# Attention and a token and channel mixer: the last addition of each sum of exponentials by an accumulating DMA, the second channel weight rounded during attention, and the first token product by seven products

## The chip, the cores and the metric

The kernel runs on one core of a Trainium2 chip. The metric is the device time of one execution in microseconds, lower is better.

The profile tells the core's work by engine, here with the instructions of each in the kernel before: TensorE (PE, 3885; its weight loads PEld, 3885), VectorE (DVE, 881), ScalarE (ACT, 707), GpSimd (POOL, 77) and SyncE (SP), which here mostly issues transfers. What it calls the DMA share is the mean busy share of sixteen DMA engines.

## The reference

Hashed attention feeds a mixer of two stages:

```python
q, k, v: (4, 8, 768, 64)      # batch, heads, sequence, head dimension
mask   = bucket(q) == bucket(k)                  # six signs of a projection
scores = where(mask, q @ k.T / 8, -1e9)
attn   = exp(scores - max) / sum                 # (768 x 768 for each head)
x      = (attn @ v) as (4, 768, 512)

h = relu(x.T @ w_tok1) @ w_tok2                  # token mixing: 768 -> 256 -> 768
u = x + h.T
out = u + relu(u @ w_ch1) @ w_ch2                # channel mixing: 512 -> 1536 -> 512
```

The mixer's four weights arrive as 64-bit numbers and are rounded to 32 bits on the chip. This document calls that a conversion.

## The kernel before

Attention handles 16 pairs of heads, one after another. A pair has two halves of 384 queries, and a half has six blocks of keys. For each block TensorE makes scores in one of three buffers (`sc`), where a product with bit rows (`bits`) does the masking. ScalarE takes the exponential of the block, and VectorE adds the six blocks of a half to `esd`, whose column sums are the denominators. Between the two halves of one pair and the scores of the next, TensorE does the previous sums, the hash of the next pair, and the weighting of the values.

```python
class Half:
    ...
    def add(self):
        self.d = pool.tile([P, 2, HALF], F32, name="esd", tag="esd", bufs=4)
        nc.vector.scalar_tensor_tensor(self.d, es[0], NR * EPS, es[1], ...)
        for e in es[2:-1]:
            nc.vector.tensor_tensor(self.d, self.d, e, op=ALU.add)
    def add_last(self):
        nc.vector.tensor_tensor(self.d, self.d, self.es[-1], op=ALU.add)

def hashes(n):                    # makes the bit rows of pair n, during pair n - 1
    ...                           # four products into hp
    nc.vector.tensor_scalar(g, ps[:, :HALF], 0.0, 0.5, op0=ALU.is_gt, op1=ALU.subtract)
    nc.scalar.mul(g, g, bitscale)
    ...                           # then eight small transfers
        nc.sync.dma_start(out=bitrows[n % 2][...], in_=g[...])

for n in range(len(pairs)):
    ...
    for now in halves:
        now.scores(); now.add()
        if now.half == 0: now.add_last()
    before.sums()
    hashes(n + 1)
    halves[1].add_last()
    load_qk(n + 2)
    add_values(n)
    weights.begin()               # ScalarE step of one conversion
    before.newton()
    weights.join()                # four VectorE steps
    halves[0].weigh()
    before.divide()
    weights.turnover()            # last VectorE step, then the load of a further weight block
    halves[1].weigh()
    if n and n % 2 == 0: bounce(...)          # stores of x, transposed, for the token stage
    if n == 2 * NP: fetch(0, x0)  # 1.5 MB: batch 0 of x comes back, after pair 8
```

Pair n + 1 cannot mask its first score block until the eight transfers of `hashes` have landed. They are issued on SyncE.

In the token stage each batch had a first product of full size, a second product by seven products, and, between them, the conversions of `w_ch2`. (Seven products means the scheme in which a product of two 2 x 2 block matrices takes seven block products instead of eight, at the price of sums.)

Of the kernel before, what the change touches and what calls it, by code (L numbers as in the profile page):

```python
# [34 lines left out]
F32 = mybir.dt.float32  # L37
BF16 = mybir.dt.bfloat16
U32 = mybir.dt.uint32
I32 = mybir.dt.int32  # L40
I64 = mybir.dt.int64
ALU = mybir.AluOpType
ACT = mybir.ActivationFunctionType
# [5 lines left out]
def kernel(  # L49
# [91 lines left out]
    class Conversion:  # L141


        def __init__(self, pool, parts, bufs):
            self.pool, self.bufs = pool, bufs
            self.todo = [
                (w, dst, rows, j, n)
                for w, dst, rows, blocks in parts
                for j in range(*blocks, rows)
                for n in range(0, dst.shape[2], NW // rows)  # L150
            ]
            self.fetched, self.begun, self.ready = [], None, None
            for _ in range(bufs - 1):
                self.fetch()
# [25 lines left out]
        def join(self):  # L180
            if not self.begun:
                return
            raw, size, to, rows = self.begun
            self.begun = None
            unit = self.pool.tile([P, NW], F32, name="unit", tag="unit", bufs=1)

            nc.vector.tensor_scalar(
                unit.bitcast(U32), size.bitcast(U32), 3, 0x7F800000,
                op0=ALU.logical_shift_left, op1=ALU.bitwise_and,
            )  # L190
            nc.vector.tensor_scalar(
                size.bitcast(U32), size.bitcast(U32), 3, None, op0=ALU.logical_shift_left,
            )

            nc.vector.scalar_tensor_tensor(unit, raw[:, :, 0], 2.0**-52, unit, op0=ALU.mult, op1=ALU.mult)  # L195
            nc.vector.tensor_tensor(size, size, unit, op=ALU.add)  # L196
            self.ready = raw, size, to, rows

        def end(self):

            if not self.ready:
                return
            raw, size, to, rows = self.ready
            self.ready = None
            hi, size = (a.rearrange("p (t n) -> p t n", t=rows) for a in (raw[:, :, 1], size.bitcast(U32)))
            nc.vector.scalar_tensor_tensor(
                to.bitcast(U32), hi, 0x80000000, size, op0=ALU.bitwise_and, op1=ALU.bitwise_or,
            )

        def turnover(self):  # L210
# [13 lines left out]

    dram = ctx.enter_context(tc.tile_pool(name="dram", bufs=1, space=bass.MemoryType.DRAM))
    bounced = [dram.tile([S, DM], F32, name=f"bounced{b}") for b in range(B)]

# [30 lines left out]
    def attention(pool, psum, W1, W2, x0):  # L258
# [63 lines left out]
        class Half:  # L322
# [54 lines left out]
            def add_last(self):  # L377
                nc.vector.tensor_tensor(self.d, self.d, self.es[-1], op=ALU.add)  # L378

# [70 lines left out]
        for _ in range(12):  # L450
# [3 lines left out]
            pool,  # L454
            [(w_tok1, W1, 3, (0, NR)), (w_tok2, W2, 1, (0, NJ)), (w_ch1, WC1, 1, (0, NCB))],
            bufs=2,
# [4 lines left out]
        for n in range(len(pairs)):  # L461
# [3 lines left out]
            for now in halves:  # L465
# [4 lines left out]
                if now.half == 0:  # L470
                    now.add_last()
            if before:
                before.sums()
# [20 lines left out]
            if before:  # L494
                before.divide()
            weights.turnover()
            halves[1].weigh()
            if n and n % 2 == 0:
# [93 lines left out]

    def tokens(pool, psum, W1, W2, x0, weights, jobs, T, places):

# [5 lines left out]
        R1 = {}  # L600
        turned = not jobs
        if not turned:
            fetch(1, x1)
            jobs = jobs(weights(pool))
            bounce(places[2], len(pairs) - 2)
        NQ = DM // 2
        sums = pool.tile([P, 3, HALF], F32, name="W2sums", tag="W2sums", bufs=1)
        b00, b01, b10, b11 = (W2[:, k, HALF * n : HALF * n + HALF] for k in range(2) for n in range(2))

        def weight_sums():  # L610
            nc.vector.tensor_tensor(sums[:, 0], b01, b00, op=ALU.subtract)
            nc.vector.tensor_tensor(sums[:, 1], b11, sums[:, 0], op=ALU.subtract)
            nc.vector.tensor_tensor(b01, b11, b01, op=ALU.subtract)
            nc.vector.tensor_tensor(sums[:, 2], b10, sums[:, 1], op=ALU.subtract)

        def job():
            if not turned and jobs:
                jobs.pop(0)()

# [3 lines left out]
        def banks():  # L623
            return psum.tile([P, 2, 512], F32, name="trp", tag="tr", bufs=2)

        def mix1(b):
            x = (x0, x1)[b % 2]
            if b and turned:
                turn(b, x, banks)
            r1 = pool.tile([P, NJ, DM], F32, name="r1", tag="r1", bufs=2)  # L630
            for j in range(NJ):
                ps = bank("t1")
                for r in range(NR):
                    nc.tensor.matmul(  # L634
                        ps, W1[:, r, P * j : P * j + P], x[:, r], start=(r == 0), stop=(r == NR - 1),
                    )
                to = r1[:, j]
                if not turned:
                    to = to.rearrange("p (c g i) -> p g c i", c=NCB, i=32)
                    ps = ps.rearrange("p (g c i) -> p g c i", c=NCB, i=32)  # L640
                nc.scalar.activation(to, ps, ACT.Relu)
                job()
            if b % 2:
# [3 lines left out]
            R1[b] = r1, new  # L647
            if not turned and b + 2 < B:
                fetch(b + 2, x)

# [11 lines left out]
        def mix2(b, m):  # L662
# [5 lines left out]
            new = new[:, :, P * m : P * m + P]  # L668
            ps = [bank("t2")[:, :HALF] for _ in range(4)]
            to = places[(2 * b + m + 1) % 3].rearrange("p (i n t) -> p i n t", i=2, n=2)  # L670
            p1, u, p7, p57 = (to[:, i, n] for i in range(2) for n in range(2))

            def product(at, left, right, start=True):
                nc.tensor.matmul(  # L674
                    ps[at], left, right, start=start, stop=True, skip_group_check=True,
                )

            product(0, a00, b00)
            nc.scalar.copy(p1, ps[0])
            product(1, a01, b10)  # L680
            product(2, s1, sums[:, 0])
            nc.scalar.copy(p57, ps[2])
            product(3, new[:, 1], b01)
            nc.scalar.copy(p7, ps[3])
            product(0, new[:, 0], sums[:, 1], False)
            nc.scalar.copy(u, ps[0])
            product(2, new[:, 2], b11, False)
            product(3, a11, sums[:, 2], False)
            nc.vector.tensor_tensor(p1, ps[1], p1, op=ALU.add)  # L689
            nc.vector.tensor_tensor(p57, p7, p57, op=ALU.add)  # L690
            nc.vector.tensor_tensor(p57, p57, u, op=ALU.add)  # L691
            nc.vector.tensor_tensor(p7, ps[3], u, op=ALU.add)
            nc.vector.tensor_tensor(u, ps[2], u, op=ALU.add)  # L693
            nc.gpsimd.dma_start(  # L694
                out=XT[:, 2 * m : 2 * m + 2, S * b : S * b + S], in_=to.rearrange("p i n t -> p i (n t)"),
                accum_op=ALU.add,
            )

        for b in range(B):
            mix1(b)  # L700
            if b == 0:
                weight_sums()
            left_sums(b)
            if b:
                mix2(b - 1, 0)
                job()
                mix2(b - 1, 1)
        mix2(B - 1, 0)
        inputs(0, T, 0)
        mix2(B - 1, 1)  # L710
        while not turned and jobs:
            job()

# [19 lines left out]
    def channels(pool, psum, SW1, second, TA, judge):  # L733
# [399 lines left out]
        def product(s, j, name, q, between, final=None):  # L1133
# [38 lines left out]
            if final:  # L1172
                issuer.dma_start(out=final(0, 0), in_=qs[:, 0])
            nc.vector.tensor_tensor(p57[:, 0], p57[:, 0], p57[:, 1], op=ALU.add)
            if j < 6 and final:
                begin(ORDER[j + 1])
            if final:
                nc.vector.tensor_tensor(qs[:, 3], qs[:, 3], u, op=ALU.add)
                nc.vector.tensor_tensor(qs[:, 3], qs[:, 3], p57[:, 0], op=ALU.add)
                issuer.dma_start(out=final(1, 1), in_=qs[:, 3])  # L1180
                for i in (1, 2):
# [177 lines left out]
    def attention_and_tokens(W1, W2, x0):  # L1359
# [12 lines left out]

        def weights(pool):
            return Conversion(pool, [(w_ch2, WC2, 3, (0, NHT))], bufs=3)

        def jobs(conversion):
            early, late = weight_sums(
                WC1, SW1, slice(0, NCB // 2), slice(NCB // 2, NCB), slice(0, DCH // 2), slice(DCH // 2, DCH),
            )
            return [  # L1380
                lambda: (early(), late()),
                *[conversion.one] * (NHT * DM // NW),
            ]

        SW2 = second["SW2"].rearrange("p i k c -> p i (k c)")
        places = [SW2[:, i] for i in range(3)]
        inside(tokens, W1, W2, x0, weights, jobs, [TA[:, 0], None, TA[:, 1], None], places)

    def careful_attention_and_tokens(W1, W2, x0):
# [11 lines left out]
        TA = big["TA"]  # L1401
        with tc.tile_pool(name="places", bufs=1, reuse_waits="tile") as pool:
            places = [pool.tile([P, 2 * S], F32, name=f"place{i}") for i in range(3)]
            inside(tokens, W1, W2, x0, None, None, [TA[:, 0], None, TA[:, 1], None], places)

# [49 lines left out]
```

## Time and profile before

| | before |
|---|---|
| time, median of 3 runs | 802.86 us (802.5 to 804.36) |
| span of the profiled run | 801.6 us |
| attention, to the first token product | 315.23 us |
| one attention pair, pairs 1 to 14 | 19.21 us each |
| token stage, first token product to first channel product | 78.53 us |
| end of the last matmul to the end | 7.05 us |

A pair's length is taken on TensorE, from the start of one pair's first score product to the start of the next pair's. It is the best ruler here: pairs do the same TensorE work, so a pair longer than 19.21 us has waited or run at a lower clock. The table and the prediction's lines show the same thing: TensorE is the bound nearly everywhere, and the chain of waits says so by engine, in shares of the span:

```profile
PE 95%; DVE 2%; DMA 1%; issue 0%; ACT 0%; DVEq 0%; ACTq 0%
```

### The profile page before, as it was taken

The page shows a single profiled execution, that of the slowest core. Times are in us where ns is not written, and L with a number is a line of the kernel's source. Part 1 is how long each engine was busy: PE and PEld are TensorE (multiplying, and loading weights), DVE is VectorE, ACT ScalarE, POOL GpSimd, SP SyncE. Part 2 cuts the span into 40 slices and gives each one's busy share as a digit, 9 for nine tenths or more (in the row PEclk, how much of TensorE's full clock was granted, in tenths as well). Part 3 has the DMA queues.
Part 4 walks back from the last instruction along what each step waited for, and adds up shares of the span by engine and source line. Part 5 has one row for each costly group of instructions (what it writes and reads, how often), then busy time and mean ns, then how long its engine had stood idle before and what let it go on. Part 6 is the DMA issues. An engine that isn't in the chain of part 4 may idle for free.

```text
span 801.6 us, 10594 instructions
## 1 busy us (share of the span) xinstructions
PE 792.5 (99%) x3885; PEld 470.6 (59%) x3885; DVE 658.0 (82%) x881; ACT 441.6 (55%) x707; POOL 53.6 (7%) x77
## 2 busy tenths in 40 slices
PE   9999999999999999999999999999999999999996
PEld 5444444444444444455544458876667886666885
DVE  4889898989887677999677888988769897779986
ACT  5688888888888886333222221327773335775111
POOL 1000000000000000011121010011110012000010
PEclk9999999999999999999999999999999999999998
DMA  4435353537352424797636994599754577630455
GB/s 163 159 122 160 121 161 122 160 121 239 128 170 90 145 72 158 199 292 177 155 69 207 305 381 169 177 299 261 235 145 145 213 201 195 214 105 9 166 179 128
DMA packets 90972, 138.61 MB, mean 173 GB/s; under 512 B 29656, under 2 KB 63392, under 8 KB 88608
## 3 DMA queue, kind: packets, MB, share of 16 engines
q1 hardware_dynamic: 82192, 112.20, 42.2%
q0 software_dynamic: 7728, 24.64, 13.8%
q10 hardware_dynamic: 992, 1.00, 0.4%
q8 instruction: 33, 0.54, 0.3%
q14 instruction: 27, 0.22, 0.1%
HBM read 97.21 MB, written 33.16 MB: 163 GB/s over the span
## 4 chain that ended last, share of the span: by engine, by line
PE 95%; DVE 2%; DMA 1%; issue 0%; ACT 0%; DVEq 0%; ACTq 0%
PE b L761 50%; PE sc L337 20%; PE acc L389 16%; PE t L634 4%; PE t L674 2%; PE sums L413 2%; DMA XT<-second 1%; PE hp L298 1%; PE hw L316 0%; PE idle L451 0%; DVE size L196 0%; DVE unit L195 0%; DVE second L693 0%; DVE second L691 0%; DVE second L689 0%
## 5 line engine op out<-in xcount | busy, mean ns | idle before, releaser
L344 ACT ACTIVATE e<-sc 128x768 f32<-128x768 f32 x192 | 154.0, 811 | 12.4 <-PE sc L337 12.0
L337 PE MATMUL sc<-qk 64*128 64x384 f32 x768 | 156.7, 487 | 0.0
L761 PE MATMUL b<-R,second 128*128 128x256 f32 (+1 forms) x612 | 150.9, 404 | 0.0
L761 PEld LDWEIGHTS b<-R,second 128*128 128x128 f32 x612 | 116.3, 190 | 31.6 <-issue 17.2
L767 ACT COPY c<-b 128x512 f32<-128x512 f32 (+1 forms) x78 | 37.5, 488 | 169.1 <-PE b L761 158.5
L389 PE MATMUL acc<-e,vn 128*64 128x384 f32 x768 | 127.6, 488 | 0.0
L375 DVE TENSOR_TENSOR esd<-esd,e 128x768 f32<-128x768 f32 x96 | 92.0, 958 | 10.0
L389 PEld LDWEIGHTS acc<-e,vn 128*64 128x64 f32 x768 | 53.6, 137 | 73.1 <-issue 71.1
L337 PEld LDWEIGHTS sc<-qk 64*128 64x128 f32 x768 | 67.5, 187 | 49.1 <-issue 47.6
L761 PE MATMUL b<-XT,WC 128*128 128x256 f32 (+1 forms) x264 | 82.5, 456 | 0.0
L761 PEld LDWEIGHTS b<-XT,WC 128*128 128x128 f32 x264 | 50.2, 190 | 29.6 <-issue 24.9
L337 PE MATMUL sc<-bits 64*128 64x384 bf16 x384 | 62.9, 323 | 0.2 <-DVE bits L320 0.2
L371 DVE SCALAR_TENSOR_TENSOR esd<-e 128x768 f32<-128x768 f32 x32 | 30.6, 955 | 28.1 <-ACT e L344 28.1
L634 PE MATMUL t<-x,W 128*128 128x512 f32 x96 | 41.8, 593 | 0.0
L395 ACT ACTIVATE num<-acc,vsum 128x384 f32<-128x384 f32 x32 | 18.6, 581 | 31.7 <-PE acc L389 31.3
L694 POOL DMA_DIRECT2D XT<-second x8 | 9.9, 1232 | 391.8 <-DVE second L693 365.9
L434 ACT COPY rec<-rec 32x384 f32<-32x384 f32 x64 | 32.6, 510 | 5.0 <-DVE rec L428 4.2
L761 PE MATMUL b<-XT,SW 128*128 128x256 f32 (+1 forms) x120 | 34.6, 422 | 0.0
L337 PEld LDWEIGHTS <-bits 64*128 64x128 bf16 x384 | 19.3, 94 | 25.4 <-DVE bits L320 0.8
L761 PE MATMUL b<-TA,WC 128*128 128x512 f32 x72 | 33.8, 592 | 0.0
L761 PE MATMUL b<-TA,SW 128*128 128x512 f32 x72 | 32.9, 592 | 0.0
L378 DVE TENSOR_TENSOR esd<-esd,e 128x768 f32<-128x768 f32 x32 | 30.5, 954 | 1.9
(214 smaller groups left out, 1131.5 us busy)
## 6 DMA issues: line engine op xcount, KB each, us to landing
second<-left SPq DMA_DIRECT2D x18, 1344.0 KB
raw<-in_moe_w_ch SPq DMA_DIRECT2D x16, 768.0 KB
qk<-in_qk SPq DMA_DIRECT2D x15, 768.0 KB
seen<-in_qk POOLq DMA_DIRECT2D x21, 384.0 KB, 4.1
WC<-hidden_left SPq DMA_DIRECT2D x15, 448.0 KB
vn<-in_v SPq DMA_DIRECT2D x16, 384.0 KB
vt<-in_vT SPq DMA_DIRECT2D x16, 384.0 KB
x<-bounced SPq DMA_DIRECT2D x4, 1536.0 KB
```

What stands on the lines that cost most here:

```text
L337: nc.tensor.matmul(sc[:, i, :HALF], t[rows, 1, P * c : P * c + P], t[rows, 0, qs], start=start, stop=not start,)
L344: nc.scalar.activation(e, sc[:, :, :HALF], ACT.Exp, scale=SCALE)
L371: nc.vector.scalar_tensor_tensor(self.d, es[0], NR * EPS, es[1], op0=ALU.add, op1=ALU.add,)
L375: nc.vector.tensor_tensor(self.d, self.d, e, op=ALU.add)
L378: nc.vector.tensor_tensor(self.d, self.d, self.es[-1], op=ALU.add)
L389: nc.tensor.matmul(acc[D * i : D * i + D], vn[:, i, c], e[:, i], start=(c == 0), stop=(c == NR - 1),)
L395: nc.scalar.activation(nums[self.n][:, self.half], acc, ACT.Identity, scale=-1.0, bias=vsum,)
L413: nc.tensor.matmul(ps[at : at + 32], ones[:, :32], self.halves[h].d[:, i], start=True, stop=True,)
L434: nc.scalar.copy(rec[other : other + 32, h], rec[at : at + 32, h])
L634: nc.tensor.matmul(ps, W1[:, r, P * j : P * j + P], x[:, r], start=(r == 0), stop=(r == NR - 1),)
L761: nc.tensor.matmul(ps, left(k), right(k), start=start and k == ks[0], stop=stop and k == ks[-1], skip_group_check=True,)
L767: nc.scalar.copy(c, ps)
```

## The change

Four things are meant to help. The first token product of batches 1 to 3 takes seven quarter products instead of eight. The conversions of `w_ch2` leave the token stage, where VectorE was 90% busy: eight more conversions run in attention, of which pairs 1, 5, 9 and 13 take a second one, and the result waits in DRAM. To pay for that, VectorE hands the last addition of each sum to an accumulating transfer (the kernel before has eight such transfers, `XT<-second`, issued on POOL, 768 KB each, with a median of 6.8 us from issue to landing). In the tail, two of the last four stores go out on SyncE. (Here and below, ` ...` marks what a cut leaves out, and the comments in the diffs are this document's.)

```diff
             def add_last(self):
-                nc.vector.tensor_tensor(self.d, self.d, self.es[-1], op=ALU.add)
+                if self.n + 1 < len(pairs):
+                    nc.gpsimd.dma_start(out=self.d, in_=self.es[-1], accum_op=ALU.add)
+                else:
+                    nc.vector.tensor_tensor(self.d, self.d, self.es[-1], op=ALU.add)
 ...
-            [(w_tok1, W1, 3, (0, NR)), (w_tok2, W2, 1, (0, NJ)), (w_ch1, WC1, 1, (0, NCB))],
+            [
+                (w_tok1, W1, 3, (0, NR)), (w_tok2, W2, 1, (0, NJ)), (w_ch1, WC1, 1, (0, NCB)),
+                (w_ch2, wc2, 3, (0, NHT)),
+            ],
 ...
                 if now.half == 0:
                     now.add_last()
+                    if n % 4 == 1:
+                        weights.one()            # a whole conversion, and the next load
 ...
             weights.turnover()
+            if n == 0:
+                weights.fetch()
 ...  # token stage, batches 1 to 3: the first product by seven
+            seven([bank("t1")[:, :NQ] for _ in range(4)], to, [
+                (u00, x00), (u01, x10), (s1, t1), (s3, x01), (s2, t2), (s4, x11), (u11, t4),
+            ])
 ...  # token stage: the converted weight comes back from DRAM
+                if b == 0:
+                    nc.sync.dma_start(out=second["WC2"], in_=wc2)
 ...  # tail
-                issuer.dma_start(out=final(0, 0), in_=qs[:, 0])
+                nc.sync.dma_start(out=final(0, 0), in_=qs[:, 0])
 ...
-                issuer.dma_start(out=final(1, 1), in_=qs[:, 3])
+                nc.sync.dma_start(out=final(1, 1), in_=qs[:, 3])
```

## The prediction

> **What bounds the kernel now.** I read the page's first line, then the kernel cut into its three stages (attention to 315.3 us, token mixing to 393.9, channel mixing to the end), then TensorE's timeline in the token stage, then one attention pair on all engines, then the last ten microseconds.
>
> ```profile
> PE 792.5 (99%) x3885; PEld 470.6 (59%) x3885; DVE 658.0 (82%) x881; ACT 441.6 (55%) x707; POOL 53.6 (7%) x77
> ```
>
> TensorE is busy for 792.5 of 801.6 us. [...] I checked the stages (columns: stretch, its length, then busy us and instructions of PE, PEld, DVE, ACT and POOL, granted clock, DMA share, GB/s):
>
> ```profile
> 0.00:315.30 315.30, 314.14 (x2201) 150.94 (x2201) 255.48 (x319) 252.81 (x377) 3.35 (x20) 1.00 0.44 143
> 315.30:393.90 78.60, 77.76 (x209) 39.61 (x210) 70.61 (x107) 28.28 (x52) 7.43 (x6) 1.00 0.78 209
> 393.90:801.60 407.70, 400.62 (x1478) 280.09 (x1476) 331.93 (x455) 160.49 (x279) 42.84 (x51) 0.99 0.63 189
> ```
>
> All of TensorE's idle time is 1.2 us at the start, 0.84 us in the token stage and 7 us after its last matmul. So the time moves only if TensorE gets fewer columns to stream, if one of those gaps closes, or if the change opens new ones.
>
> ```profile
> 315.23 20.87 PE L634 MATMUL t<-x,W 128*128 128x512 f32 x48
> 364.29 10.46 PE L634 MATMUL t<-x,W 128*128 128x512 f32 x24
> 374.59 1.45 PE L674 MATMUL t<-W,r 128*128 128x384 f32 x4
> 391.72 0.91 PE L674 MATMUL t<-W2sums,r1s 128*128 128x384 f32 x2 [0.84 <-ACT second L679]
> ```
>
> From start to start, a first token product takes 374.59 - 364.29 = 10.30 us, or 429 ns for each of 24 records (the trace shows two records for each float32 matmul). The channel stage's 256-wide records take (789.18 - 784.65) / 21 = 216 ns in the last stretch:
>
> ```profile
> 784.65 4.70 PE L761 MATMUL b<-R,second 128*128 128x256 f32 x21
> 789.18 1.46 PE L761 MATMUL b<-second,second 128*128 128x256 f32 x6
> 793.96 1.63 ACTq L1180 DMA_DIRECT2D out<-second  x1
> 794.56 0.76 DVE L1184 TENSOR_TENSOR second<-b,second 128x256 f32<-128x256 f32 x2
> 795.68 1.23 ACTq L1185 DMA_DIRECT2D out<-second  x2
> ```
>
> [...] the trace of one pair shows twelve exponentials in 9.67 us, back to back. [...] the eight of before are on POOL, 768 KB each, with a median of 6.8 us from issue to landing. [...]
>
> **The change, part by part.**
>
> *First token product by seven products.* Batch 0 stays whole, in two column halves: 48 records x 216 = 10.36 us instead of 10.30, so +0.06. Batches 1 to 3 take seven of eight quarter products, each of three k-blocks: 21 matmuls, 42 records, 9.07 us instead of 10.30. Three times -1.23 is -3.7 us on TensorE, which is the path. Net: **-3.6 us**.
>
> VectorE pays 4 weight sums of 384 columns (0.55 us), 12 input sums of 768 (0.96) and 15 combining additions of 256 (0.42): about 20 us. Taking eight conversions out of the stage (two of 0.56, three of about 0.96: 4.0 us each) frees 32. VectorE falls from 70.6 to about 59 of some 74 us, so it still does not bound the stage. I walked its order: the sums for batch 1 are the tight ones. The last conversion ends near 317, and batch 1's input is now requested behind its store, at about 317.4 instead of 305.7 (in times of before). Packet records show that 1.5 MB takes about 4 us at 390 GB/s, so it lands near 324; TensorE wants it at 325.6. The VectorE sums run from 325.7 to 329.6, just in front of the products that want them (third product at 328.2, fourth at 329.5). I expect no stall, but the margin is one to two microseconds.
>
> *The gap at 391.* ScalarE waited there for an accumulating transfer to leave a buffer. That transfer was issued at 381.3 because VectorE was busy with a conversion, and took 9.8 us beside weight loads. Both causes leave the stage: **-0.8 us**.
>
> *Second weight rounded in attention.* Conversions there go from 12 to 20, one in each of 16 pairs and a second one in pairs 1, 5, 9 and 13. This is +8 x 4.0 = 32 us for VectorE, paid by *the last addition by DMA*, which removes 30 x 0.954 = 28.6 us. So VectorE is hardly relieved in total (255.5 becomes about 259 us) and what counts is order. In the twelve other pairs an addition goes and nothing else comes before the hash: they keep their slack. In the four special pairs a whole conversion stands between the two halves. Pair 5 in the kernel before:
>
> ```profile
> 104.78 9.67 ACT L344 ACTIVATE e<-sc 128x768 f32<-128x768 f32 x12 [0.44 <-PE sc L337]
> 106.41 0.96 DVE L371 SCALAR_TENSOR_TENSOR esd<-e 128x768 f32<-128x768 f32 x1 [0.60 <-ACT e L344]
> 110.66 0.96 DVE L378 TENSOR_TENSOR esd<-esd,e 128x768 f32<-128x768 f32 x1
> 115.59 0.55 DVE L302 TENSOR_SCALAR g<-hp 128x384 bf16<-128x384 f32 x1
> 116.18 0.62 ACT L303 ACTIVATE g<-g,bitscale 128x384 bf16<-128x384 bf16 x1 [0.68 <-DVE g L302]
> 116.82 5.91 SPq L308 DMA_DIRECT2D bits<-g  x8
> 123.60 0.33 PE L337 MATMUL sc<-bits 64*128 64x384 bf16 x2
> ```
>
> First, ScalarE: exponentials come every 0.806 us and score blocks every 0.807, with three score buffers. A 0.92 us conversion step after the sixth exponential puts the end of the seventh at 1.14 + 7 x 0.806 + 0.92 = 7.70 us after the start of the scores; TensorE wants that buffer for the tenth block at 7.37. With about 0.08 for the semaphore it waits 0.41 us. Nothing makes that up later: four times is **+1.6 us**.
>
> Second, the hash: VectorE trades a 0.87 us addition for a 4.0 us conversion, so the step that starts at 115.59 starts 3.1 us later. The eight bit transfers follow 0.73 us apart. In the packet records of before, the fourth ends at 120.57 and the eighth at 123.50; 3.1 us later is 123.7 and 126.6. The next pair's first bit product (123.60) has moved to 124.0 by the first stall and wants the first four: met. Its fourth block, 2.4 us on, wants the last: 126.4 against 126.7 with the semaphore. About 0.25 us of wait, four times: **+1.0 us**.
>
> The accumulating transfers land within some 5 us of issue (estimated from 6.8 us for twice the size), the sums are read more than 10 us later, and the last pair keeps its addition, so those waits are hidden. DMA share in attention rises from 0.44: in the packet records the eight old accumulating transfers move 200 GB/s with all 16 engines busy, so 384 KB is 2 us, two a pair in 19.2: +0.2, plus weights: about 0.7.
>
> *The tail.* The last product's four stores were all issued on ScalarE, three of them in the fence of the last stretch above. The 1.63 us issue holds up the third store, whose data are there at 795.0, until 795.68. With the first two on SyncE that is gone: **-0.6 us**.
>
> Sum: -3.6 - 0.8 + 1.6 + 1.0 - 0.6 = -2.4, and 802.9 - 2.4 is about 800.4 us.
>
> **The rivals.**
> 1. *Attention takes it without stalls.* For it: the slack of bits is over 2 us in every pair now, and the stalls I get are differences of a few tenths. Against it: exponentials and score blocks have the same pace, so a 0.92 us insertion cannot be absorbed by three buffers. It would give 797.8.
> 2. *The bits get later than I think.* The second accumulating transfer of a special pair leaves just with the bit transfers and takes all 16 engines for 2 us; small packets queue behind 3 KB ones. Another 0.5 to 1.5 us in each special pair, and perhaps in others, gives 803 to 807. Against it: the bits are paced by SyncE at 0.73 us and only the last is critical.
> 3. *The token stage turns VectorE-bound or waits for its input,* as batch 1 is fetched 12 us later, behind a store: each microsecond late is a microsecond. It would give 801 to 804. For it: VectorE was 90% busy there; against it: 12 us less work on it and the margins above.
>
> **Range and chances.** The gains are counted columns and measured gaps, firm within a microsecond; the losses in attention are worth 0 to 6. So 800.3 us, 8 times in 10 within 797 to 804. Two per cent is 16 us: no part of the change is that large, so faster 0.01, same 0.97, slower 0.02.
>
> **What would show it.** Right: TensorE's busy time 3.5 us down or nearly; in the token stage no gap, and second to fourth first-product groups of 9.07 us; two gaps in each special pair and the one after it (0.4 us at the tenth block behind an exponential, some tenths at a bit product), none in the other pairs. Wrong: special pairs as long as the others at 19.21 us (rival 1), gaps above 1 us at bit products (rival 2), or gaps before the first product of batch 1 (rival 3).

## The result, and the profile after

| | before | after |
|---|---|---|
| median of 6 runs each | 803.61 us (802.5 to 805.58) | 810.83 us (808.04 to 812.62) |
| ratio | | 1.0089, 95% interval 1.0065 to 1.0113 |

A ratio here and below is the mean time of one kernel's runs over the mean of the other's runs of the same rounds, so it is not quite the ratio of the medians quoted beside it. The kernel is 0.9% slower: "within 2%", but slower, and outside the range of 797 to 804.

The profiled execution is the fastest of the six, 808.04 us with a span of 805.9. What follows is an account of that one run; the other five were up to 4.6 us longer.

First the page of the kernel after: busy time by engine, the chain of waits by engine, and the issues of the accumulating transfer (last columns: number, KB each, median us from issue to landing).

```profile
PE 793.4 (98%) x3963; PEld 491.1 (61%) x3963; DVE 647.6 (80%) x882; ACT 443.6 (55%) x721; POOL 79.7 (10%) x107
...
PE 87%; DVE 4%; DMA 4%; SPq 2%; ACT 1%; issue 1%; DVEq 0%; ACTq 0%
...
esd<-e POOLq DMA_DIRECT2D x30, 384.0 KB, 5.1
```

TensorE was to lose about 3.5 us of busy time and has gained 0.9. The chain, which was 95% TensorE, now leaves it for VectorE, DMA and SyncE's issues for a tenth of the span: new waits. Where they are, the same three stretches tell (columns as in the prediction):

```profile
0.00:326.30 326.30, 318.87 (x2201) 156.45 (x2201) 258.21 (x328) 256.17 (x384) 29.62 (x50) 0.99 0.69 195
326.30:400.10 73.80, 73.80 (x289) 54.47 (x288) 59.40 (x99) 27.02 (x59) 7.25 (x6) 1.00 0.80 223
400.10:805.90 405.80, 400.69 (x1478) 280.16 (x1476) 330.04 (x456) 160.38 (x279) 42.82 (x51) 1.00 0.62 189
```

The token stage is what was wanted: TensorE is busy in all of it. Attention is 11 us longer with the same 2201 matmuls. In it TensorE idles 326.30 - 318.87 = 7.4 us, against 1.2 before, and is busy 4.7 us longer for the same work.

| stage | before | after | difference |
|---|---|---|---|
| to the first token product | 315.23 | 326.24 | +11.0 |
| token stage | 78.53 | 73.78 | -4.75 |
| first channel product to last matmul | 400.76 | 400.77 | 0.0 |
| after the last matmul | 7.05 | 5.1 | -1.9 |
| span | 801.6 | 805.9 | +4.3 |

Attention's 11.0 us split by pair. Every pair not named took as long as before (19.21 us; pair 0 20.99 and pair 15 19.50); the part ahead of pair 0 became 0.5 us shorter.

| pair | length after, us | above 19.21 | what TensorE waited for |
|---|---|---|---|
| 1 | 20.36 | +1.15 | a score buffer, held by the second conversion's ScalarE step, whose weight block had not landed |
| 5, 9, 13 | 19.47 each | +0.26 each | a score buffer, held by the conversion's ScalarE step |
| 2, 6 | 20.00, 20.02 | +0.79, +0.81 | bits |
| 14 | 20.70 | +1.49 | bits |
| 10 | 25.70 | +6.49 | bits; then it ran at half the clock |

The sum is 11.5, and 11.5 - 0.5 is the 11.0 of the stage table. So one pair makes more than half of the loss.

Pair 5 and the start of pair 6 in the timeline after (start, duration, engine, line, operation, tiles; in brackets the idle time before and who ended it), against the same stretch in the prediction:

```profile
110.94 0.92 ACT L181 ACTIVATE size<-raw 128x768 f32<-128x768 f32 x1
...
119.88 0.55 DVE L313 TENSOR_SCALAR g<-hp 128x384 bf16<-128x384 f32 x1
120.47 0.61 ACT L314 ACTIVATE g<-g,bitscale 128x384 bf16<-128x384 bf16 x1 [3.27 <-DVE g L313]
...
121.11 6.08 SPq L319 DMA_DIRECT2D bits<-g  x8
...
128.35 0.51 PE L348 MATMUL sc<-bits 64*128 64x384 bf16 x2 [0.35 <-DMA bits<-g]
```

Pair 5's scores start at 105.08 here and at 103.64 before. The hash step comes 14.80 us after that start instead of 11.95, so 2.85 us later. This is the order of work that the prediction foresaw, and TensorE then waits at the bits. The ScalarE conversion step stands among the exponentials at 110.94.

Pair 9 does the same work, but its end looks different:

```profile
198.52 0.87 POOL L391 DMA_DIRECT2D esd<-e  x1 [7.09 <-DVE g L313]
199.02 9.15 SPq L319 DMA_DIRECT2D bits<-g  x8
207.25 0.68 PE L348 MATMUL sc<-bits 64*128 64x384 bf16 x2 [3.89 <-DMA bits<-g]
```

The eight bit transfers take SyncE 9.15 us from the first issue to the end of the last instead of some 6 (with two pauses, of 1.4 and 1.9 us, before the last two), and TensorE stands still for 3.89 us. The windows around that gap show what lies beside it (columns as above; the last three are granted clock, DMA share and GB/s):

```profile
203.00:205.00 2.00, 0.37 (x4) 0.00 (x0) 2.00 (x3) 0.81 (x2) 0.00 (x0) 1.00 1.08 253
205.00:207.00 2.00, 0.00 (x0) 0.00 (x0) 0.45 (x1) 0.00 (x0) 0.00 (x0) 0.55 0.43 140
...
209.00:211.00 2.00, 2.00 (x12) 1.47 (x10) 0.59 (x1) 0.81 (x1) 0.00 (x0) 0.50 0.78 129
```

The wait costs twice. The DMA engines are full until about 205, then they empty, and the bits land. After that TensorE's granted clock stays at 0.50 until 212: the clock records show 0.50 from 205.20 to 212.03, beginning 1.83 us after TensorE had gone idle at 203.37. Half clock followed shorter waits in other runs too, 1.94 us in x_parts and 1.87 us in accum_only (below). From 207.25 to 212 at half the rate, some 2.4 us of work are lost (an estimate from these windows). With the 3.89 us that is nearly all of pair 10's 6.49.

Why are the DMA engines full? Pair 9 cut into four windows, in the kernel before and then after:

```profile
180.48:184.50 4.02, 4.02 (x32) 2.27 (x32) 3.29 (x5) 3.46 (x5) 0.00 (x0) 1.00 0.75 223
184.50:189.50 5.00, 5.00 (x42) 2.89 (x40) 4.58 (x6) 4.98 (x7) 0.00 (x0) 1.00 1.15 297
189.50:194.50 5.00, 5.00 (x42) 1.95 (x40) 4.76 (x7) 4.29 (x9) 0.00 (x0) 1.00 0.98 301
194.50:199.69 5.19, 5.19 (x35) 2.09 (x31) 5.12 (x8) 3.41 (x6) 0.00 (x0) 1.00 0.46 174
```

```profile
187.00:192.00 5.00, 5.00 (x38) 2.65 (x36) 4.72 (x7) 5.00 (x8) 0.89 (x1) 1.00 1.21 301
192.00:197.00 5.00, 5.00 (x42) 2.06 (x40) 4.65 (x6) 3.07 (x5) 0.00 (x0) 1.00 0.90 224
197.00:202.50 5.50, 5.50 (x38) 2.22 (x34) 4.63 (x8) 4.06 (x8) 0.87 (x1) 1.00 1.05 354
```

Read the DMA share, the last number but one. Already before, this pair filled the DMA engines for ten microseconds, because batch 0 of x (1.5 MB) comes back after pair 8, behind the ordinary loads. What saved it were the last 5 us with a share of 0.46, in which the bits travelled. After the change two accumulating transfers and a second weight block lie in the pair, the share is 1.05 at its end, and no such stretch is left. In the packet records the bits, first issued at 199.02, have their first packets only at about 205. They come behind the 2 KB packets of earlier loads in the same queue, with the 3 KB packets of the accumulating transfer in between: from 199.02 to the first bit packet at 205.26, 443 packets of 2 KB and 256 plain ones of 3 KB start in the bits' queue, and 132 of the accumulating transfers in the other.

The records also give the price of accumulating: a 3072-byte packet of `esd<-e` takes 0.252 us, a plain packet of that size 0.121. So 128 packets on 16 engines are 2.0 us of all sixteen.

In the tail, the line to compare with the prediction's 1.63 us issue is the second; it no longer stands in front of the third store:

```profile
800.22 0.33 SPq L1266 DMA_DIRECT2D out<-second  x1
...
801.28 1.03 ACTq L1271 DMA_DIRECT2D out<-second  x2
```

### The profile page after: what moved, and what is told of

It reads as the page before. It is cut to its first block, busy times and chain, and to the rows that moved or that the text cites. A ratio compares the mean times of both kernels' runs of the same rounds, so it can differ in the third digit from the quotient of the medians. Undisturbed runs are those within 1.5% of the kernel's fastest.

```text
span 805.9 us, 10891 instructions
## 1 busy us (share of the span) xinstructions
PE 793.4 (98%) x3963; PEld 491.1 (61%) x3963; DVE 647.6 (80%) x882; ACT 443.6 (55%) x721; POOL 79.7 (10%) x107
## 4 chain that ended last, share of the span: by engine, by line
PE 87%; DVE 4%; DMA 4%; SPq 2%; ACT 1%; issue 1%; DVEq 0%; ACTq 0%
PE b L847 50%; PE sc L348 14%; PE acc L404 11%; PE t L666 8%; DMA bits<-g 2%; SPq L319 2%; DVE esd L386 2%; PE t L711 1%; DMA raw<-in_moe_w_tok 1%; DMA raw<-in_moe_w_ch 1%; PE sums L428 1%; PE hp L309 1%; DVE esd L382 1%; ACT e L355 1%; DVE size L200 0%
## 5 line engine op out<-in xcount | busy, mean ns | idle before, releaser
L348 PE MATMUL sc<-qk 64*128 64x384 f32 x768 | 160.4, 494 | 0.9 <-ACT e L355 0.9
L386 DVE TENSOR_TENSOR esd<-esd,e 128x768 f32<-128x768 f32 x96 | 92.0, 958 | 11.0 <-ACT e L355 1.3
L348 PEld LDWEIGHTS sc<-qk 64*128 64x128 f32 x768 | 70.5, 189 | 48.1 <-issue 40.7
L348 PE MATMUL sc<-bits 64*128 64x384 bf16 x384 | 67.5, 326 | 5.5 <-DMA bits<-g 5.4
L391 POOL DMA_DIRECT2D esd<-e x30 | 26.3, 876 | 270.3 <-ACT e L355 105.2
L348 PEld LDWEIGHTS <-bits 64*128 64x128 bf16 x384 | 22.8, 95 | 32.1 <-DMA bits<-g 9.3
L847 PEld LDWEIGHTS b<-XT,SW 128*128 128x128 f32 x120 | 22.8, 190 | 10.8 <-issue 7.0
L1025 ACT ACTIVATE R<-R 128x1024 f32<-128x1024 f32 x24 | 24.4, 1054 | 3.5 <-DVE R L1022 3.5
```

Source lines behind the costliest of these rows:

```text
L348: nc.tensor.matmul(sc[:, i, :HALF], t[rows, 1, P * c : P * c + P], t[rows, 0, qs], start=start, stop=not start,)
L391: nc.gpsimd.dma_start(out=self.d, in_=self.es[-1], accum_op=ALU.add)
L847: nc.tensor.matmul(ps, left(k), right(k), start=start and k == ks[0], stop=stop and k == ks[-1], skip_group_check=True,)
L1025: nc.scalar.activation(r[i], r[i], ACT.Relu)
```

## The experiments

Two theories stood against each other. *Order*: the second conversion stands ahead of the hash in VectorE's order, so the bits are late; move it, and the loss goes. *Queues*: the bits travel too slowly, because accumulating transfers, weight blocks and the 1.5 MB of x fill the DMA engines just then; move or remove a transfer, and the loss goes. The expectations name shares of each: their "theory Q" blames VectorE's order and the freed load in the bits' own queue, "rival D" the accumulating transfers, and "theory Q2", from x_parts on, full DMA engines where the 1.5 MB and the accumulating transfers meet. There were twelve kernels in three batches; each batch has runs of the kernel before on the same chip (batches 1 and 2 on one chip, batch 3 on another). All twelve computed the right result.

| batch | before, median us |
|---|---|
| 1: late_extra, late_fetch, x_later, accum_only | 803.11 (7 runs) |
| 2: x_parts, vector_last, spread, tail_only | 803.13 (8 runs) |
| 3: spread_whole, spread_vector, spread_vector_whole, accum_parts | 803.29 (7 runs) |

Diffs are against the kernel after, if not said otherwise. Pair lengths are those of the one profiled run.

### late_extra: the second conversion behind the hash

```diff
                 if now.half == 0:
                     now.add_last()
-                    if n % 4 == 1:
-                        weights.one()
 ...
             load_qk(n + 2)
+            if n % 4 == 1:
+                weights.one()
             add_values(n)
```

> The second conversion of pairs 1, 5, 9 and 13 is moved behind the hash of the next pair, and its weight load with it. Theory Q (the bits of the next pair are late because a conversion of VectorE stands before the hash and the load that it frees stands before the bits in the same queue): all pairs go back to 19.21 us, at most 0.3 more in the pair after a special one; token stage 73.9 us; 797 to 799 us, faster than before. Rival D (the accumulating transfers load the DMA engines so that the bits are late anyway): pairs 2, 6, 10 and 14 stay 0.8 us or more too long, 803 us or more.

Measured: 812.43 us (811.25 to 814.76), ratio 1.0119 (1.0095 to 1.0144). Theory Q failed. The numbers of rival D came true, but its cause, late bits, only in part. Pairs 1, 5, 9 and 13 take 19.21 us, so the first term of the prediction is gone, but the pairs behind them lose more: 20.41 us for pair 2, 20.42 for pairs 6 and 14, 23.61 for pair 10. Pair 12 takes 20.13, pair 0 22.22 (a late first load), and pair 15 takes 24.01 instead of 19.50. In pairs 10 and 15 TensorE waits for bits, 2.42 and 2.53 us, and then runs at half the clock for 3.41 us; in pairs 2, 6 and 14 it waits for a score buffer. The reason for these three stands in the timeline:

```profile
46.24 0.94 ACT L181 ACTIVATE size<-raw 128x768 f32<-128x768 f32 x1 [3.25 <-DVE W L213]
...
50.50 0.92 PE L348 MATMUL sc<-qk 64*128 64x384 f32 x4 [0.93 <-ACT num L410]
```

Two conversions in a row make ScalarE wait 3.25 us for VectorE to be done with the first one's tile. ScalarE's next steps come late by that, among them the one that reads the score buffer (`num`), and TensorE waits for that buffer. A later place in VectorE's order is not free: the conversion has a step on ScalarE, and that engine's order carries the wait on.

### late_fetch: only the load of the next weight block behind the hash

```diff
                     if n % 4 == 1:
-                        weights.one()
+                        weights.begin()
+                        weights.join()
+                        weights.end()
 ...
             load_qk(n + 2)
+            if n % 4 == 1:
+                weights.fetch()
             add_values(n)
```

> The second conversion stays between the halves, only the load that it frees is issued behind the bits. If the queue in front of the bits is the larger cause: pair 10 falls from 25.7 us to about 20.0, pair 14 from 20.7 to about 20.0, pairs 2 and 6 stay at 20.0 (VectorE is still 3.1 us late); some 804 us. If only VectorE's lateness counts: pair 10 stays above 24 us and the time at 810 us.

Measured: 807.27 us (806.75 to 808.17), ratio 1.0056 (1.0039 to 1.0073). That is 3.6 us better than after by the medians (810.83 of an earlier set of runs). The order on VectorE is unchanged; only a 768 KB transfer has moved out of the way of the bits. Pair 10 falls from 25.70 to 20.86. The total stays 3 us above the 804 expected, since the first two pairs are worse (24.26 and 21.0 us): in the profiled run TensorE waits 1.85 us in pair 0 for a late initial load and then runs at half the clock for 3.41 us, and in pair 1 it waits 1.52 us for a score buffer. This speaks for queues as the cause of the large wait.

### x_later: the 1.5 MB of x two pairs later

```diff
-            if n == 2 * NP:
+            if n == 2 * NP + 2:
                 fetch(0, x0)
```

> As the changed kernel, but the first token input (1.5 MB) is fetched two pairs later, after pair 10 instead of pair 8, so that it does not meet a pair with a second conversion. If it is the 1.5 MB that fill the queue in front of the bits of pair 10: pair 10 falls from 25.7 to about 20.0 us, some 805 us. If it is the accumulating transfers or the second weight load alone: pair 10 stays above 22 us, 808 us or more.

Measured: 809.97 us (808.09 to 810.73), ratio 1.0078 (1.006 to 1.0097). Pair 10 falls to 19.78 us, as expected, but pair 12 rises to 26.39, with a wait of 3.98 us for bits, so the expected 805 us did not come. The long wait moved with the transfer. Pairs 11 and 12 have no second conversion in front of them, so the wait needs none. That is against order as its cause.

### accum_only: the kernel before, with the accumulating transfers alone

```diff
  (against the kernel before)
             def add_last(self):
-                nc.vector.tensor_tensor(self.d, self.d, self.es[-1], op=ALU.add)
+                if self.n + 1 < len(pairs):
+                    nc.gpsimd.dma_start(out=self.d, in_=self.es[-1], accum_op=ALU.add)
+                else:
+                    nc.vector.tensor_tensor(self.d, self.d, self.es[-1], op=ALU.add)
```

> The kernel before with nothing but the last addition by accumulating DMA. Theory Q: the hash starts 0.2 us earlier, the transfers are hidden, all pairs 19.21 us, 803.6 us within 1. Rival D: the 30 transfers make the bits or loads late, pairs longer than 19.3 us, 806 us or more.

Measured: 807.1 us (807.7, 806.95, 807.26 and 802.6), ratio 1.0032 (1.0 to 1.0063). I had expected no change, and by the medians that was wrong, though the interval reaches down to 1.0. Nothing is converted between the halves here, the hash is where it was, VectorE has less to do, and still pair 10 takes 23.11 us. The chain of waits of that stretch, and the window ahead of it:

```profile
194.84 7.50 DMA bits<-g
...
202.39 4.62 PE sc L337 x20
```

```profile
195.00:200.00 5.00, 5.00 (x32) 2.17 (x30) 4.62 (x6) 2.83 (x6) 0.00 (x0) 1.00 1.07 276
```

Though the hash is not behind a second conversion here, a bit transfer spends 7.50 us on its way, and the DMA share at the end of pair 9 is 1.07 where it was 0.46. One of the four runs, at 802.6, is as fast as before, which suggests that the wait is near its edge and does not come in every run, or not in full.

### x_parts: the 1.5 MB in six parts, after pairs 8 to 13

```diff
-            if n == 2 * NP:
-                fetch(0, x0)
+            if 2 * NP <= n < 2 * NP + NR:
+                r = slice(n - 2 * NP, n - 2 * NP + 1)
+                nc.sync.dma_start(out=x0[:, r], in_=bounced[0].rearrange("(r p) c -> p r c", p=P)[:, r])
```

> As the changed kernel, but the first token input is fetched in six parts, one behind each of pairs 8 to 13, instead of 1.5 MB at once. Theory Q2 (the queue in front of the bits is full in the pair that also has the 1.5 MB, since the accumulating transfers have taken the room that was left): pair 10 falls from 25.7 us to 20.5 or less, pair 12 does not rise as it did with the later fetch; 804 to 806 us. Rival (the second weight load of pair 9 alone): pair 10 above 22 us, 809 us.

Measured: 807.01 us (806.78 to 807.76), ratio 1.0052 (1.0035 to 1.0069). Pair 10 is at 19.82; no pair reaches 25. The time is 1 us above the 804 to 806 expected. What is left is 20.32 for pair 1, 19.85 and 20.06 for pairs 2 and 6, 19.72 for pair 12, and 23.19 for pair 14. So 256 KB a pair costs little where there is no second conversion. Pair 14, behind the special pair 13, still waits 1.94 us for its bits, and loses 4 us in all, since the clock is at half behind this wait as well:

```profile
283.72 0.51 PE L348 MATMUL sc<-bits 64*128 64x384 bf16 x2 [1.94 <-DMA bits<-g]
...
285.14 1.62 PE L348 MATMUL sc<-qk 64*128 64x384 f32 x4
```

Four matmul records that take 0.81 us elsewhere take 1.62. The clock records show 0.50 from 284.47 for 3.41 us, which costs some 1.7 us (an estimate).

### vector_last: the kernel after, with all last additions on VectorE

```diff
-                if self.n + 1 < len(pairs):
-                    nc.gpsimd.dma_start(out=self.d, in_=self.es[-1], accum_op=ALU.add)
-                else:
-                    nc.vector.tensor_tensor(self.d, self.d, self.es[-1], op=ALU.add)
+                nc.vector.tensor_tensor(self.d, self.d, self.es[-1], op=ALU.add)
```

> As the changed kernel, but the last addition is done by VectorE again. VectorE starts the hash of special pairs 0.9 us later still. Theory Q2: pair 10 falls below 23 us as the queues are emptier, pairs 2, 6 and 14 rise from 20.0 to about 20.9; 807 to 811 us. If the accumulating transfers cost nothing: pair 10 rises to 26.5 us, 814 us or more.

Measured: 804.94 us (804.62 to 805.14), ratio 1.0022 (1.0005 to 1.0039). That is below both forecasts. Taking the accumulating transfers out of the kernel after makes it 5.9 us faster by the medians (of two sets of runs, 810.83 and 804.94; the ratios to before are 1.0089 and 1.0022). The special pairs, pair 1 among them, take 19.46 or 19.47, and pairs 2, 6, 10 and 14 are all alike at 20.7: with fewer transfers in the queues each loses the same 1.5 us, pair 10 included. That much comes from order. In this kernel the addition after the first half stands ahead of the hash on VectorE again (0.95 us, the row of the prediction); without it about 0.55 us would be left (an estimate), which is near the 0.8 of pairs 2 and 6 in the kernel after. So order has a share of its own, more than the 0.25 predicted, but it does not make 6.49.

### spread: the extra conversions moved, x in six parts

```diff
+        EXTRA = (2, 4, 6, 8)
 ...
-                    if n % 4 == 1:
-                        weights.one()
+                    if n in EXTRA:
+                        weights.turnover()       # the last step of the extra one
 ...
+            if n + 1 in EXTRA:
+                weights.turnover()
+                weights.begin()                  # the extra one starts behind the hash, a pair earlier
             if before:
                 before.divide()
-            weights.turnover()
+            if n + 1 not in EXTRA:
+                weights.turnover()
             if n == 0:
                 weights.fetch()
+            if n + 1 in EXTRA:
+                weights.join()
             halves[1].weigh()
 ...  # and the edit of x_parts
```

> As the parts above, and the second conversion moved: its ScalarE step into the pause between the two outputs at the end of the pair before, its first four VectorE steps at the start of pairs 2, 4, 6 and 8 (where VectorE waits for the second exponential), its last step and its load between the halves. The hash is then 0.7 us later than before, within its slack. Theory Q2: all pairs 19.21 us within 0.1, the token stage 73.8 us, 796 to 798 us, faster than both kernels. Rival (the accumulating transfers delay bits in any pair): several pairs over 19.5 us, 800 us or more.

Measured: **798.96 us** (798.67 to 799.76), ratio 0.995 (0.9933 to 0.9967). It beats both kernels: 0.5% faster than before, which by a limit of 2% still counts as the same. It is 1 us more than the 796 to 798 expected. TensorE never stops for bits: all pairs take their 19.21 us (pair 15 its 19.50) but pair 0 (21.61, for its first load) and pair 12 (19.4, where a weight load waits 0.4 us for bits). From its page the busy times and the chain, then the window at the end of pair 9:

```profile
PE 788.5 (99%) x3963; PEld 486.6 (61%) x3963; DVE 649.4 (81%) x882; ACT 446.3 (56%) x721; POOL 79.6 (10%) x107
...
PE 98%; DMA 1%; DVE 0%; issue 0%; ACTq 0%
```

```profile
195.00:200.00 5.00, 5.00 (x34) 2.08 (x30) 4.66 (x6) 2.86 (x6) 0.00 (x0) 1.00 0.70 182
```

TensorE's busy time is 4 us below that of before, about the cut that was counted in columns, and the chain is 98% TensorE. The DMA share is 0.70 where it was 1.05.

### tail_only: the kernel before, with the two stores on SyncE

```diff
  (against the kernel before)
-                issuer.dma_start(out=final(0, 0), in_=qs[:, 0])
+                nc.sync.dma_start(out=final(0, 0), in_=qs[:, 0])
 ...
-                issuer.dma_start(out=final(1, 1), in_=qs[:, 3])
+                nc.sync.dma_start(out=final(1, 1), in_=qs[:, 3])
```

> The kernel before with nothing but the last product's first two stores issued by SyncE. My prediction was 0.6 us less, the two traces suggest 1.9 us (6.26 us from the end of the last addition to the end of the span before, 4.3 us after). Expected: 801.5 us. If the end only varies from run to run: no change.

Measured in five rounds: 802.43 us (801.99 to 803.01), ratio 0.9991 (0.9978 to 1.0005). The interval holds 1, so a gain is not shown; 0.7 us by the medians fits the predicted 0.6 better than the 1.9 that one profile seemed to show. From the start of the last row of matmuls to the end, the eleven profiles of kernels with the new tail took 9.16 us (after) to 11.02 (x_parts), 10.2 in the mean; the three with the old one took 10.91 (accum_parts), 11.09 (before) and 11.61 (accum_only). So the 9.16 of the profile after was the luckiest of eleven draws.

### spread_whole, spread_vector, spread_vector_whole: which part of spread matters

spread_whole leaves out the edit of x_parts; spread_vector keeps it but has the last additions on VectorE (the edit of vector_last); spread_vector_whole has its additions on VectorE and x at once.

```diff
  (against spread: spread_whole and spread_vector_whole)
-            if 2 * NP <= n < 2 * NP + NR:
-                ...
+            if n == 2 * NP:
+                fetch(0, x0)
  (against spread: spread_vector and spread_vector_whole)
-                    nc.gpsimd.dma_start(out=self.d, in_=self.es[-1], accum_op=ALU.add)
+                nc.vector.tensor_tensor(self.d, self.d, self.es[-1], op=ALU.add)
```

> The spread version with the 1.5 MB token input fetched at once again (accumulating transfers kept). Theory Q2: pair 10 waits for its bits as in the kernel with the accumulating transfers alone (23.1 us instead of 19.21), 802 to 804 us. If the moved conversions alone had cured it: 799 us as spread.

> The spread version with the last addition on VectorE again, token input in six parts. The hash of the four even pairs starts some 1.6 us later than before, within its slack of 2.4. If VectorE never needed the relief: all pairs 19.21 us, 798.5 to 799.5 us, the same as spread. If it did: pairs 2, 4, 6, 8 over 19.5 us, 801 us or more.

> Last addition on VectorE and the token input at once, with the conversions spread. Theory Q2: without the accumulating transfers the queues empty in time as they did before the change, all pairs 19.21 us, 798.5 to 799.5 us. If the 1.5 MB at once are enough by themselves to delay the bits beside the eight more weight loads: pair 10 above 20 us, 801 us or more.

| with the conversions of spread | x in six parts | x at once |
|---|---|---|
| last addition by accumulating DMA | 798.96 (0.995) | 804.2 (1.0007, interval 0.9982 to 1.0033) |
| last addition on VectorE | 801.24 (0.9967, interval 0.9942 to 0.9992) | 802.26 (0.9976, interval 0.9949 to 1.0003) |

Medians in us, in brackets the ratio to before. By the medians the accumulating DMA gains 2.3 us with x in parts (801.24 - 798.96), and loses 1.9 us with x at once. All runs of the two kernels in parts lie apart (at most 799.76 against at least 800.83), though they are of two batches and two chips; the two at once share a batch, and the intervals of their ratios overlap. So the gain is fairly sure, the loss less so; that the one becomes the other suggests that the operation is neither good nor bad by itself. It gained where there was room in the DMA engines (a share of 0.70 from 195 to 200 us in spread) and not where there was none (1.03 in the same window of spread_whole). By the expectations: spread_whole came as theory Q2 said. spread_vector came near its second case (801.24, with pairs 4, 6 and 8 over 19.5 us, but not pair 2). spread_vector_whole went against theory Q2: pair 10 takes 20.09 us, waiting for bits, so the 1.5 MB at once cost 0.9 us there even without accumulating transfers; pairs 4, 6, 8 and 9 are long (19.63 to 20.11) much as in spread_vector.

The runs of spread_whole were 801.1, 804.24, 805.04 and 804.17; the profile is of the mildest, with 22.99 us for pair 10. TensorE's wait for bits there was 3.44 us, and the granted clock stayed at 1.00 in all windows from 198 to 212 us. So 3.44 us did not cost the clock, where 1.94 us in x_parts did, and 1.87 us in accum_only.

The clock records hint at why. In the kernel after, half clock starts at 205.20 and at 805.95, which is 176.0 steps of 3.413 us apart, and its first stretch, 6.83 us, is two such steps. In accum_only it starts at 202.76 and at 803.51, again 176.0 steps apart. If the clock changes at such steps alone, the wait of accum_only lies whole in one of them (199.35 to 202.76), and that of spread_whole is cut into 1.77 and 1.66 us. This is my estimate from the clock records of these traces, made after the fact; no run tested it, and none set where in a step a wait falls.

What VectorE's addition costs shows in spread_vector: pair 4 takes 19.64 us and pairs 6, 8 and 9 take 20.1. In pair 9 TensorE waits 0.52 us for bits; in the others its wait is for a buffer that ScalarE reads late:

```profile
125.54 0.92 PE L348 MATMUL sc<-qk 64*128 64x384 f32 x4 [0.63 <-ACT num L407]
```

### accum_parts: the kernel before, with the accumulating transfers, and x in six parts

The edit is that of accum_only and of x_parts, both against the kernel before.

```diff
  (against accum_only)
-            if n == 2 * NP:
-                fetch(0, x0)
+            if 2 * NP <= n < 2 * NP + NR:
+                r = slice(n - 2 * NP, n - 2 * NP + 1)
+                nc.sync.dma_start(out=x0[:, r], in_=bounced[0].rearrange("(r p) c -> p r c", p=P)[:, r])
```

> The kernel before with the accumulating transfers alone and the token input in six parts. Theory Q2: the wait of pair 10 that the accumulating transfers alone gave (23.1 us) is gone, all pairs 19.21 us, 803 us as before. If the accumulating transfers delay bits wherever: some other pair over 19.5 us, 805 us or more.

Measured: 802.87 us (802.08 to 803.43), ratio 0.9986 (0.996 to 1.0012); no pair after the first (21.60, for its first load) is longer than before, pair 10 included. With accum_only this settles the cause of pair 10's long wait: the accumulating transfers make it only beside the 1.5 MB at once, and neither the further conversions nor the order on VectorE is needed for it.

## Why the prediction was wrong

**First token product, -3.6 us: right.** Batch 0 took 10.47 us instead of the 10.36 worked out, and batches 1 to 3 took 9.06 or 9.07 instead of 9.07, which makes -3.64. VectorE's busy time in the stage is 59.40 us, as worked out (about 59), and there is no wait for the input of batch 1. Rival 3 is refuted. All ten profiles of kernels with the seven products show a token stage of 73.77 or 73.78 us.

**The gap at 391, -0.8: right.** It is gone and was worth 1.1 us from start to start. With the term above that makes the stage's -4.75.

**First, ScalarE, +1.6: right in sum, by luck in part.** The loss to the buffer wait was 0.26 us in pairs 5, 9 and 13 instead of 0.41. (The 0.08 us for the semaphore was my estimate; in pair 5 after, 0.05 us pass from the end of the exponential at 112.56 to the product's start at 112.61.) Pair 1 lost 1.15, because the weight block of its extra conversion had not landed: the chain of waits spends 10.36 us on that one transfer.

```profile
22.64 10.36 DMA raw<-in_moe_w_tok
```

Together 1.15 + 3 x 0.26 = 1.93 us. That an early load might be late was in none of my rivals.

**Second, the hash, "About 0.25 us of wait, four times: +1.0 us": this is the step that failed.** Its first half held: the hash came 2.85 us later in pair 5 (I said 3.1, taking 0.87 us for an addition that my own line shows at 0.96). Its second half took the time from the issue of the bits to their landing from the kernel before, and let it stay the same. It did not: the pairs lost 0.79, 0.81, 6.49 and 1.49 us, together 9.58. Where the DMA engines had room the error was half a microsecond. Behind pair 9 they had none.

I had even counted the load: two transfers of 2 us a pair. But I added it to an average ("+0.2, plus weights: about 0.7"; measured 0.69 for attention) and called the transfers hidden because their own result is read late. An average of 0.69 looks like room. What counted is what was queued ahead of a small transfer that the path waits for, in the one pair where the kernel before had only 5 us left with a share of 0.46. Rival 2 named the mechanism and the range of 803 to 807, but allowed each pair 0.5 to 1.5 us, and argued that SyncE's issues pace the bits. In pair 9 they did not: the issues themselves stretched from 5.91 us (pair 5 of before) to 9.15, and the first packets came 6 us after the first issue. And no rival had the half clock, which turned 3.9 us of waiting into 6.5.

**The tail, -0.6: about right**, as far as five rounds can tell.

**The sum.** (802.9 - 2.4 is 800.5; the recorded text writes 800.4 and then 800.3.) Replacing the failed term alone, 802.9 - 2.4 - 1.0 + 9.6 gives 809.1 us, and the profiled run was at 808.04. The median of 810.83 is higher still. That the runs differ so much more than those of spread (798.67 to 799.76) fits waits that depend on how queues meet in a run; as profiles show one run each, this is argued and not shown.

**What is shown and what is not.** Shown, by accum_only, x_later, x_parts and accum_parts: the long wait of pair 10 comes from accumulating transfers and 1.5 MB at once in the same pair. In the kernel after, the second weight load ahead of the bits adds to it: taking away any one of the three leaves pair 10 at 20.73 us (vector_last), 19.82 (x_parts) or 20.86 (late_fetch). Shown, by spread: without those waits the change gives 0.5%, -4 us or so, near what rival 1 gave for an attention without stalls (797.8). Open: why the median lies above the profiled run, why bits were 1.9 to 2.5 us late without the 1.5 MB in pair 14 of x_parts and pair 15 of late_extra, and how the long wait splits between the two queues' packets, since no run changed the queue or size of the accumulating transfer alone.

## What to carry to other kernels

Before traffic is moved to the DMA engines to relieve an engine, look for the smallest transfer that the critical path waits for, and read the DMA share in the windows between its issue and its landing, in every repetition and not on average. A large transfer without a deadline can be cut into parts over several iterations: by the medians, with the conversions of spread, that alone turned the accumulating addition from a loss of 1.9 us into a gain of 2.3. And look at the granted clock behind a TensorE gap, which can cost more than its length: 1.87 us (accum_only) and 1.94 us (x_parts) were each followed by 3.41 us at half the clock, while 3.44 us (spread_whole) were not.
